# A build-time scheduler's durations set to traced ones, and wider gates for its vector banks

## The chip, the cores and the metric

The kernel runs on one core of a Trainium2 chip. The metric is the device time of one execution in microseconds. A difference is judged against the kernel before, run on the same chip. Five engines work side by side, each with its own in-order queue: TensorE (PE, matmuls), VectorE (DVE), ScalarE (ACT), GpSimd (POOL) and SyncE (SP, which issues transfers). They wait for each other through semaphores.

## The reference, cut to what matters

One transformer block with modulation: layer norm, attention with 32 heads of 16 over 2048 tokens, then a gated feed-forward. All inputs are bf16.

```python
mod = (silu(c) @ w_mod).reshape(1, 6, 1, 512)       # sa, ca, ga, sb, cb, gb
h = layernorm(x) * (1 + ca) + sa                    # x: 1 x 2048 x 512
q, k, v = split(h @ wqkv, 32 heads of 16)
p = softmax(q @ k.T * 16 ** -0.5)                   # 32 x 2048 x 2048
x = x + ga * ((p @ v) @ wo)
h = layernorm(x) * (1 + cb) + sb
x = x + gb * ((gelu(h @ w_gate) * (h @ w_up)) @ w_down)   # 512 -> 1792 -> 512
```

## The kernel before

**Tiling.** The scores are made transposed, keys on the 128 partitions and queries along the free dimension, in banks of 128 x 512 fp32. There are 32 x 2048 x 2048 / 65536 = 2048 such banks. `qk` writes them into six PSUM banks (`ps_sc`) used as two halves of three. Four matmuls of 32 rows (one for each of four heads) run side by side. The queries are cut into seven sets (`SETS`: 512, 512, 256, 256, 256, 128, 128), and a unit is one set and one of eight groups of four heads. `pv_round` multiplies four finished banks with the values and a column of ones into `ps_pv`, so that the row sums come out along with the products.

**Two ways for an exponential.** ScalarE takes two or three banks in one activation, `E<-ps_sc` with 1024 or 1536 elements. DVE can take a single bank, called a vector bank here, in the seven operations of `exp_vec`: `dt<-ps_sc` frees the PSUM bank; `dx<-dt` reads every second 16-bit word of `dt`; then come two `TENSOR_SCALAR`, two `TENSOR_TENSOR` and a last `SCALAR_TENSOR_TENSOR`. In the profile they write `ed`, `mreg` or `qT`, whose unused parts hold the results. Where a vector bank is taken, ScalarE's activation has 1024 elements in place of 1536.

**Side work.** Projections, output projection and feed-forward run in between as side work. They all go through a single PSUM bank (`ps_mi`), which DVE has to empty (L329, L334, L338) before the next group of matmuls may write it. The tanh of gelu runs on ScalarE (`wreg<-wreg`, 512 or 1024 elements, 37 times). When a unit has its last round, its sums go through DRAM (`scr_den`, `scr_rec`): SP issues a transfer out and one in, DVE takes the reciprocal (`rden<-den`), SP writes it out and issues four broadcasts into `rb`; DVE then multiplies (`onorm<-osb,rb`).

**What sets the order.** Every engine's order is fixed when the program is built. `rec` (L167) records each operation with the waits that it needs, and `model` (L244) gives it a start and an end in a planned time, from the durations of `cost` (L283); a transfer has its own durations in `model`. `probe` (L273) asks when an operation could start in that planned time. The loop in `stream` (L1069) decides with these planned times what PE does next: scores (`qk`), values (`pv_round`), a step of side work (`advance`), or a filler matmul that keeps PE busy. `background` (L986) and `step` hand DVE its next task when the plan says DVE is free. A wrong duration does not make a wrong result, since the semaphores hold; it makes another order.

**The gates of a vector bank** stand in `stream` (L1163 to L1166): fewer than `NACT` = 3 active ones, fewer than `BACK` = 8 DVE steps in the `backlog`, DVE planned free within 700 ns, and `credit`, the side work that is overdue in matmul columns, below 1024. `credit` grows with every group of scores and falls with each step of side work.

**The end.** `tail` (L1338) runs the feed-forward of the last two sets when all exponentials are given out. Before it, `side_ffn` with `EARLY` = 2 does the first two chunks of the second-last set (up-projection, tanh, product), and `near_end` (L841) forms the last sums on PE (`ps_mi<-osb,self`, `ps_sc<-osb,self`) with a reciprocal straight from PSUM (`rb<-ps_mi`, `rb<-ps_sc`). Then come the output projection of the last 128 tokens (`ps_sc<-wo,onorm`), its layer norm (`st<-ps_sc` and ten small operations), up- and down-projections and the last transfer out.

Of the kernel before, what the change touches and what calls it, by code (L numbers as in the profile page):

```python
# [38 lines left out]
CH = 3  # L39
# [6 lines left out]
NED = 6  # L46
LAG = 60
EARLY = 2
BACK = 8
SOON = 100  # L50
END = (0, None)

# [11 lines left out]
class _Op:  # L64
    __slots__ = ("eng", "stream", "seq", "fn", "inc", "waits", "clock", "tag", "t1")

    def __init__(self, eng, stream, seq, fn):
        self.eng = eng
        self.stream = stream
        self.seq = seq  # L70
        self.fn = fn
        self.inc = False
        self.waits = {}
        self.clock = None
        self.tag = None


class _Recorder:
# [88 lines left out]
    def rec(self, eng, fn, reads=(), writes=(), dma=None, cost=0.0):  # L167

        if self.dry:
            return None  # L170
        stream = eng if dma is None else "d_" + dma
        seq = self.count.get(stream, 0) + 1
        needs = {}

# [37 lines left out]
        if self.probing is not None:  # L212
            self.probing = max(self.probing, at)
            return None
        self.count[stream] = seq
        op = _Op(eng, stream, seq, fn)
        self.bystream.setdefault(stream, []).append(op)
        ck = self.clock[eng]
# [11 lines left out]
        for w, name, kind, bxs in acc:  # L230
            h = self.hist.setdefault(name, {})
            for b in bxs:
# [4 lines left out]
                else:  # L237
                    h.setdefault(b, [None, {}])[1][stream] = seq
        self.ops.append(op)
        self.model(op, max(at, self.free[eng]), cost)  # L240
        return op


    def model(self, op, t, cost):  # L244
        eng = op.eng
        if op.stream not in COMPUTE:
            self.free[eng] = t + 50
            self.dma_free = max(t + 1400, self.dma_free) + cost / 350
            op.t1 = self.dma_free + 1000
        elif eng == "pe":  # L250
            cols, rows, tp = cost
            mode = 0 if tp is None else (1 if rows == 32 else 2)
            t = max(t, self.pe_issue)
            if mode != self.pe_mode:
                t = max(t, self.pe_end + 105)
            q = range(16)
            if mode == 1:
                q = range(tp[0] // 8, tp[0] // 8 + 4)
            elif mode == 2:
                q = range(tp[1] // 32, 16, 4)  # L260
            t = max(t, max(self.tile_free[i] for i in q))
            end = t + max(cols, 64) / 2.4
            for i in q:
                self.tile_free[i] = end
            self.pe_mode, self.pe_issue, self.pe_end = mode, t + (4 if mode else 27), max(self.pe_end, end)
            self.free[eng] = t
            self.log.append((t, cols if mode == 0 else cols / 4))
            op.t1 = end + 158
        else:
            self.free[eng] = t + cost  # L270
            op.t1 = t + cost + (107 if eng == "act" else 92)
# [11 lines left out]
    def cost(self, eng, out, ins, kind):  # L283
        n = 1
        for _, k in (out if kind != "bn" else ins[0]).ap[1:]:
            n *= int(k)
        aps = [out] + list(ins)
        ps = any(self.kind.get(a.tensor.name) == "ps" for a in aps)
        small = all(mybir.dt.size(a.dtype) == 2 for a in aps)
        if eng == "act":  # L290
            return n * 0.833 + (60 if ps else 92)
        if eng == "pool":
            return n * 3.0 + 100
        f = 1
        if not ps:
            f = {("ts", True): 4, ("ts", False): 2, ("tt", True): 2}.get((kind, small), 1)
        return n * 1.042 / f + 65

    def mm(self, out, lhsT, rhs, start=True, stop=True, tp=None):
        n = 1  # L300
# [23 lines left out]
    def ts(self, eng, out, a, s1, s2, op0, op1=None):  # L324
        kw = {"op0": op0}
        if op1 is not None:
            kw["op1"] = op1
        rd = [a] + [s for s in (s1, s2) if isinstance(s, bass.AP)]
        return self.rec(eng, lambda e: e.tensor_scalar(out, a, s1, s2, **kw), rd, [out],  # L329
                        cost=self.cost(eng, out, [a], "ts"))  # L330

    def stt(self, out, a, s, b, op0, op1):
        rd = [a, b] + ([s] if isinstance(s, bass.AP) else [])
# [5 lines left out]

    def recip(self, out, in_):  # L340
        return self.rec("dve", lambda e: e.reciprocal(out, in_), [in_], [out],
                        cost=6.25 * self.cost("dve", out, [in_], "stt"))

    def memset(self, eng, ap, val, after=()):
        return self.rec(eng, lambda e: e.memset(ap, val), after, [ap], cost=self.cost(eng, ap, [], "ts"))
# [63 lines left out]
class _Kernel(_Recorder):  # L409
# [659 lines left out]
    def stream(self):  # L1069
# [39 lines left out]
        def take(n):  # L1109
            r, i = [], pos  # L1110
            while len(r) < n and i < nseq:
                if i not in vec:
                    r.append(i)
                i += 1
            return r, i
# [18 lines left out]
        while rp < len(rounds):  # L1134
# [5 lines left out]
            t = max(self.pe_now(), virt)  # L1140
# [7 lines left out]
            mem, after = take(CH - 1 if pos < nsplit + 12 and c % 2 else CH)  # L1148
# [5 lines left out]
            if tq is not None and tq <= t + 30:  # L1154
                slack = self.free["act"] - 600 - t
                w = self.next_side()
                if w is not None and pos >= w[1] and self.credit > 1536 and slack > 213 and self.probe(w[4][1]) <= t:
                    self.advance()
                    continue
                if self.short(t) > (0 if slack > 213 else DIRE) and slack > 0:  # L1160
                    self.mm(self.scp[:, s0, :], *filler)
                    continue
                g = None  # L1163
                if (('v', 3, 0) in self.have and len(active) < NACT and sum(v >= 4 * rp for v in vec) < NED
                        and self.backlog() < BACK and self.free["dve"] < t + 700
                        and len(mem) == CH and slack > -100 and self.credit < 1024):  # L1166
                    g = pos + CH * LEAD
                    g += 3 - g % 4
                    while g in vec:
                        g += 4  # L1170
                    if g >= nseq - 4 * LEAD or any(k not in self.have for k in self.keys(seq[g])):
                        g = None
                if g is not None:
                    vec.add(g)
                    mem, after = take(CH - 1)
                items = [(m, s0 + i) for i, m in enumerate(mem)]
                if g is not None:
                    items.append((g, s0 + len(mem)))
                self.require(sorted({k for m, _ in items for k in self.keys(seq[m])}))
                self.qk([(seq[m], k) for m, k in items])  # L1180
                n = len(mem)
                while self.step("act", self.free["act"]):
                    pass
                self.act(self.E[:, e0:e0 + n, :], self.scp[:, s0:s0 + n, :], ACT.Exp, scale=EXP_SCALE)
                for i, m in enumerate(mem):
                    owner[e0 + i] = rof[m]
                    self.slot[m] = self.E[:, e0 + i, :]
                if g is not None:
                    out = self.ED[pos >= ends[0]][nd % NED]
                    if pos < ends[0]:  # L1190
                        low.add(g)
                    steps = self.exp_vec(nd, self.scp[:, s0 + n, :], c % 2, out)
                    self.task(steps[:1], ("ld", nd), first=True)
                    self.task(steps[1:], ("exp", nd), self.after([("ld", nd)]))
                    active.append((("exp", nd), g, out))
                    nd += 1
                if self.work and pos >= self.work[0][1]:
                    w = self.work[0]
                    rate = w[3] / max(1, w[2] - pos)
                    self.credit = min(self.credit + rate * len(items), 4096)  # L1200
                pos, e, c = after, e0 + n, c + 1
                continue
# [4 lines left out]
            ts = None  # L1207
            side = False
            if w is not None and pos >= w[1]:
                ts = self.probe(w[4][1])  # L1210
                n = w[4][0]
# [13 lines left out]
            if self.short(t) > (0 if gap > 213 else DIRE) and not self.open and gap > 0 and self.probe(  # L1225
                    lambda: self.mm(self.mi[:, :], *filler)) <= t + 30:
                self.mm(self.mi[:, :], *filler)
                continue
            nxt = [x for x in (tq, tp[0], tp[1], ts) if x is not None and x > t + 30]
            if self.tasks:  # L1230
                nxt.append(max(self.free["dve"], t + 100))
# [251 lines left out]
```

## Time and profile before

| what | us |
|---|---|
| median of 3 runs | 917.43 (916.13 to 919.24) |
| the profiled execution | 915.94 |
| its span, first to last instruction | 914.2 |
| DVE busy | 817.3 (89%) |
| ScalarE (ACT) busy | 881.1 (96%) |
| PE busy | 798.2 (87%) |

The profile's rows are read like this. A group's row has the line, the engine, the operation, what it writes from what, the shape, and the count after an x; then the busy time of the group in us, the mean of one in ns, and the idle time before them with what ended it. A timeline's row has the start and the length in us. A row of the windows has the busy time of each engine in that stretch, and near its end the clock that TensorE was granted, as a share of full speed. An engine's instructions can overlap by some tenths of a microsecond, so the distance between two starts, not the length of one, is what an instruction costs its queue.

### The profile page before, as it was taken

What the parts mean: (1) busy time and instruction counts of PE and PEld (TensorE: products, weight loads), DVE (VectorE), ACT (ScalarE), POOL (GpSimd) and SP (SyncE); (2) the same over time, 40 slices, a digit from 0 to 9 for tenths busy, and PEclk for the clock granted to TensorE, in tenths of its full rate; (3) what the DMA queues carried; (4) which work ended last, traced back from release to release, by engine and by line L of the source; (5) the groups of instructions that cost most, each with busy time, mean ns of one, the idle gap of its engine ahead of it and who ended that gap; (6) DMA issues with size and microseconds to landing.
All of it is one profiled execution on the core that took longest, in us unless ns stands there. A gap on an engine that the chain in (4) does not pass through costs nothing.

```text
span 914.2 us, 20663 instructions
## 1 busy us (share of the span) xinstructions
PE 798.2 (87%) x8563; PEld 289.3 (32%) x8697; DVE 817.3 (89%) x2065; ACT 881.1 (96%) x754; POOL 3.6 (0%) x11
## 2 busy tenths in 40 slices
PE   8898888888888888888888888889888988898878
PEld 3332322222222222222223222333333333234455
DVE  8757999999997999999997997998999899988874
ACT  6999999999999999999999999999999999999991
POOL 1000000000000000000000000000000000000000
PEclk9999999999999999999999999999999999999999
DMA  9003210000100000000000000000000000000000
GB/s 299 1 24 94 101 47 14 13 14 13 54 13 13 2 13 15 13 14 25 9 25 14 14 8 14 14 26 19 9 15 19 16 12 12 22 15 14 23 6 13
DMA packets 35336, 25.18 MB, mean 28 GB/s; under 512 B 19053, under 2 KB 31082, under 8 KB 35242
## 3 DMA queue, kind: packets, MB, share of 16 engines
q1 hardware_dynamic: 32858, 22.28, 8.4%
q10 hardware_dynamic: 2384, 1.57, 0.6%
q8 instruction: 68, 1.11, 0.5%
q14 instruction: 26, 0.21, 0.1%
HBM read 21.23 MB, written 2.61 MB: 26 GB/s over the span
## 4 chain that ended last, share of the span: by engine, by line
DVE 43%; ACT 42%; PE 9%; DMA 3%; issue 2%; SPq 1%; DVEq 0%
ACT E L317 40%; DVE dt L329 7%; DVE dx L329 4%; PE ps_sc L304 4%; PE ps_mi L304 4%; DVE qT L321 3%; DVE qT L329 3%; DVE qT L334 3%; DVE ed L321 3%; DVE mreg L321 2%; DVE ed L334 2%; DVE mreg L334 2%; DVE ed L329 2%; DMA rb<-scr_rec 2%; DVE wreg L334 2%
## 5 line engine op out<-in xcount | busy, mean ns | idle before, releaser
L317 ACT ACTIVATE E<-ps_sc 128x1536 bf16<-128x1536 f32 (+2 forms) x698 | 852.7, 1390 | 13.8 <-PE ps_sc L304 13.0
L304 PE MATMUL ps_pv<-E,vaug 128*17 128x256 bf16 (+2 forms) x2922 | 182.6, 300 | 4.8 <-DVE osb L338 2.1
L304 PE MATMUL ps_sc<-qT,kme 32*128 32x256 bf16 (+2 forms) x1600 | 167.8, 304 | 21.3 <-ACT E L317 15.4
L304 PE MATMUL ps_sc<-qT,kmo 32*128 32x256 bf16 (+2 forms) x1664 | 167.6, 298 | 17.4 <-ACT E L317 12.6
L329 DVE TENSOR_SCALAR dt<-ps_sc 128x512 int32<-128x512 f32 x182 | 123.8, 682 | 10.4 <-PE ps_sc L304 9.5
L304 PE MATMUL ps_mi<-wreg,mreg 128*128 128x256 bf16 (+2 forms) x603 | 117.9, 306 | 11.9 <-DVE wreg L338 4.1
L304 PE MATMUL ps_sc<-kme,ident 128*128 128x512 bf16 x300 | 98.0, 383 | 32.9 <-ACT E L317 28.7
L304 PEld LDWEIGHTS ps_sc<-qT,kme 32*128 32x128 bf16 x1600 | 47.7, 92 | 130.6 <-ACT E L317 74.2
L304 PEld LDWEIGHTS ps_sc<-qT,kmo 32*128 32x128 bf16 x1664 | 49.4, 92 | 120.1 <-ACT E L317 66.7
L304 PEld LDWEIGHTS ps_pv<-E,vaug 128*17 128x17 bf16 x2922 | 53.4, 88 | 100.7 <-issue 86.7
L329 DVE TENSOR_SCALAR dx<-dt 128x512 f16<-128x512 uint16 x182 | 75.4, 418 | 0.1
L321 DVE TENSOR_TENSOR qT<-qT,dx 128x512 f16<-128x512 f16 x180 | 73.6, 416 | 1.2
L304 PEld LDWEIGHTS ps_mi<-wreg,mreg 128*128 128x128 bf16 x624 | 47.4, 97 | 61.8 <-issue 27.4
L334 DVE SCALAR_TENSOR_TENSOR qT<-dt,qT 128x512 int16<-128x512 int32 x90 | 61.5, 683 | 0.3
L304 PE MATMUL ps_mi<-dreg,hreg 128*128 128x512 bf16 x180 | 56.4, 384 | 3.2 <-issue 1.6
L321 DVE TENSOR_TENSOR ed<-ed,dx 128x512 f16<-128x512 f16 x124 | 51.0, 416 | 0.6
L304 PEld LDWEIGHTS ps_sc<-kme,ident 128*128 128x128 bf16 x342 | 24.9, 97 | 83.7 <-ACT E L317 77.2
L338 DVE CAST wreg<-ps_mi 128x512 bf16<-128x512 f32 x51 | 35.0, 685 | 16.7 <-PE ps_mi L304 16.5
L334 DVE SCALAR_TENSOR_TENSOR ed<-dt,ed 128x512 int16<-128x512 int32 x62 | 42.1, 681 | 0.4
L321 DVE TENSOR_TENSOR wreg<-wreg 128x512 bf16<-128x512 bf16 (+1 forms) x74 | 38.5, 520 | 0.9
L304 PE MATMUL ps_mi<-hreg,wreg 128*128 128x512 bf16 x107 | 35.0, 385 | 3.6 <-DVE qT L329 2.2
L334 DVE SCALAR_TENSOR_TENSOR wreg<-wreg,ps_mi 128x512 bf16<-128x512 bf16 x51 | 34.7, 680 | 1.8 <-PE ps_mi L304 1.5
(131 smaller groups left out, 740.8 us busy)
## 6 DMA issues: line engine op xcount, KB each, us to landing
rb<-scr_rec SPq DMA_DIRECT2D x64, 64.0 KB, 2.0
rb<-scr_rec SPq DMA_DIRECT2D x116, 32.0 KB, 1.8
mreg<-in_w_mod_dram SPq DMA_DIRECT2D x1, 2048.0 KB, 14.1
out_dram<-xs SPq DMA_DIRECT2D x16, 128.0 KB, 1.7
mreg<-in_B_w_gate_dram SPq DMA_DIRECT2D x4, 448.0 KB, 4.0
mreg<-in_B_w_up_dram SPq DMA_DIRECT2D x4, 448.0 KB, 6.1
dreg<-in_B_w_down_dram SPq DMA_DIRECT2D x3, 512.0 KB, 3.9
wreg<-in_A_wqkv_dram SPq DMA_DIRECT2D x3, 384.0 KB, 10.6
```

What stands on the lines that cost most here:

```text
L304: return self.rec("pe", lambda e: e.matmul(out, lhsT, rhs, start=start, stop=stop, tile_position=tp), [lhsT, rhs], [out], cost=(n, int(rhs ...
L317: return self.rec("act", lambda e: e.activation(out, in_, func, scale=scale, **kw), rd, wr, cost=self.cost("act", out, [in_], "act"))
L321: return self.rec(eng, lambda e: e.tensor_tensor(out, a, b, op), [a, b], [out], cost=self.cost(eng, out, [a, b], "tt"))
L329: return self.rec(eng, lambda e: e.tensor_scalar(out, a, s1, s2, **kw), rd, [out], cost=self.cost(eng, out, [a], "ts"))
L334: return self.rec("dve", lambda e: e.scalar_tensor_tensor(out, a, s, b, op0=op0, op1=op1), rd, [out], cost=self.cost("dve", out, [a, b], " ...
L338: return self.rec(eng, lambda e: e.tensor_copy(out, in_), [in_], [out], cost=self.cost(eng, out, [in_], "ts"))
```

## The change

It touches only numbers of the planner; no operation of the kernel has another form, and no transfer is added.

- `small` in `cost`: an operand counts as 16-bit and dense only if its last step is 1. Before, the type alone decided.
- ScalarE: 51 or 93 ns of fixed cost in place of 60 or 92.
- DVE: 68 ns of fixed cost in place of 65; a new kind `col` for an operation with scalars read per partition, planned at 0.52 ns an element and 190 ns from PSUM in 16 bit, 1.042 ns and 128 ns from PSUM otherwise, and at half rate in SBUF.
- The reciprocal: 360 ns less.
- Transfers: issuing on SP takes 430 ns in place of 50; the transfer starts 800 ns after the issue in place of 1400.
- Gates: `BACK` 10 in place of 8; `credit` below 2600 in place of 1024.

```diff
-BACK = 8
+BACK = 10
...
         if op.stream not in COMPUTE:
-            self.free[eng] = t + 50
-            self.dma_free = max(t + 1400, self.dma_free) + cost / 350
+            self.free[eng] = t + (430 if eng == "sp" else 50)
+            self.dma_free = max(t + 800, self.dma_free) + cost / 350
             op.t1 = self.dma_free + 1000
...
-        small = all(mybir.dt.size(a.dtype) == 2 for a in aps)
+        small = all(mybir.dt.size(a.dtype) == 2 and int(a.ap[-1][0]) == 1 for a in aps)
         if eng == "act":
-            return n * 0.833 + (60 if ps else 92)
+            return n * 0.833 + (51 if ps else 93)
         if eng == "pool":
             return n * 3.0 + 100
         f = 1
+        if ps and kind == "col":
+            return n * 0.52 + 190 if small else n * 1.042 + 128
         if not ps:
-            f = {("ts", True): 4, ("ts", False): 2, ("tt", True): 2}.get((kind, small), 1)
-        return n * 1.042 / f + 65
+            f = {("ts", True): 4, ("ts", False): 2, ("col", True): 2, ("tt", True): 2}.get((kind, small), 1)
+        return n * 1.042 / f + 68
...
-                        cost=self.cost(eng, out, [a], "ts"))
+                        cost=self.cost(eng, out, [a], "ts" if len(rd) == 1 else "col"))
...
-                        cost=6.25 * self.cost("dve", out, [in_], "stt"))
+                        cost=6.25 * self.cost("dve", out, [in_], "stt") - 360)
...
-                        and len(mem) == CH and slack > -100 and self.credit < 1024):
+                        and len(mem) == CH and slack > -100 and self.credit < 2600):
```

## The prediction

> **What bounds the kernel now.** I read the page's busy shares first, then the windows of the stretch between the first and the last softmax exponential, then ScalarE's groups by shape and its timeline, and last who waited for whom.
>
> ```profile
> span 914.2 us, 20663 instructions
> PE 798.2 (87%) x8563; PEld 289.3 (32%) x8697; DVE 817.3 (89%) x2065; ACT 881.1 (96%) x754; POOL 3.6 (0%) x11
> 15.26:888.59 873.33, 765.08 (x8259) 269.84 (x8386) 793.02 (x1996) 868.01 (x729) 0.31 (x1) 1.00 0.08 23
> 100.00:250.00 150.00, 129.82 (x1009) 39.23 (x1025) 148.46 (x366) 148.72 (x125) 0.00 (x0) 1.00 0.11 31
> 450.00:700.00 250.00, 221.63 (x2768) 78.76 (x2812) 227.88 (x575) 249.03 (x208) 0.00 (x0) 1.00 0.06 16
> ```
>
> In the window rows the columns are length, then busy time of PE, weight loads, DVE and ACT. ScalarE works 868.0 of the 873.3 us from first to last exponential; DVE has 873.3 - 793.0 = 80.3 us idle there, but almost none from 100 to 250. So the end is set by ScalarE's queue, plus a head of 15.3 us and a tail of 914.2 - 888.6 = 25.6 us. What ScalarE's queue holds:
>
> ```profile
> L317 ACT ACTIVATE E<-ps_sc 128x1536 bf16<-128x1536 f32 x482 | 688.3, 1525 | 4.0 <-PE ps_sc L304 3.4
> L317 ACT ACTIVATE E<-ps_sc 128x1024 bf16<-128x1024 f32 x210 | 229.3, 1105 | 1.2 <-PE ps_sc L304 1.0
> L317 ACT ACTIVATE wreg<-wreg 128x512 bf16<-128x512 bf16 x23 | 16.6, 722 | 0.0
> L317 ACT ACTIVATE wreg<-wreg 128x1024 bf16<-128x1024 bf16 x14 | 15.5, 1104 | 0.7 <-DVE wreg L321 0.7
> ```
>
> ```profile
> 15.26 3.71 ACT L317 ACTIVATE E<-ps_sc 128x1536 bf16<-128x1536 f32 x3 [0.58 <-PE ps_sc L304]
> ...
> 879.32 5.57 ACT L317 ACTIVATE E<-ps_sc 128x1536 bf16<-128x1536 f32 x4
> 884.64 0.76 ACT L317 ACTIVATE wreg<-wreg 128x512 bf16<-128x512 bf16 x1
> ...
> 886.50 0.76 ACT L317 ACTIVATE wreg<-wreg 128x512 bf16<-128x512 bf16 x1
> 887.01 1.58 ACT L317 ACTIVATE E<-ps_sc 128x1536 bf16<-128x1536 f32 x1
> ```
>
> Instructions on ScalarE overlap, so the mean of one is not what it costs the queue. Four 1536-wide ones from 879.32 to 884.64 are 5.32 / 4 = 1.330 us each, 0.195 less than their mean. The 1024-wide one, 420 ns shorter in the mean, is 0.910 us; the tanh of 512 takes 887.01 - 886.50 = 0.51, that of 1024 by the same overlap 0.91. The queue's work is 482 x 1.330 + 210 x 0.910 + 23 x 0.51 + 14 x 0.91 = 856.6 us. The stretch lasts 873.3, so 16.7 us are lost to exponentials that start late. Those 16.7 and the count of banks are all that the planner can move in this stretch.
>
> ```profile
> ACT E L317 <- PE ps_sc L304: 4.4, 12, 0.6
> PE ps_mi L304 <- DVE wreg L334: 6.6, 14, 0.8
> PE ps_mi L304 <- DVE xw L321: 4.6, 12, 0.7
> PE ps_mi L304 <- DVE wreg L338: 4.1, 11, 0.7
> DVE onorm L321 <- DMA rb<-scr_rec: 5.9, 9, 1.3
> ```
>
> ```profile
> 147.21 0.74 DVE L329 TENSOR_SCALAR kmo<-ps_mi,rm 128x512 bf16<-128x512 f32 x1
> 148.00 0.40 PE L304 MATMUL ps_mi<-wreg,hreg 128*128 128x128 bf16 x4 [0.72 <-DVE kmo L329]
> 148.77 2.79 ACT L317 ACTIVATE E<-ps_sc 128x1536 bf16<-128x1536 f32 x2 [0.54 <-PE ps_sc L304]
> ```
>
> The waits (us in all, times, longest) say where a visible part comes from, and the three rows at 148 show one whole case. PE's queue is in order. The planner put projection matmuls where it thought DVE had already emptied the one side bank; DVE had not, PE stood 0.72 us, the scores behind it were late, and ScalarE stood 0.54 us.
>
> **The change part by part.** Planned durations first. One vector bank is seven DVE operations, and here seven run without a gap:
>
> ```profile
> 156.22 0.68 DVE L329 TENSOR_SCALAR dt<-ps_sc 128x512 int32<-128x512 f32 x1
> 156.82 0.68 DVE L334 SCALAR_TENSOR_TENSOR mreg<-dt,mreg 128x512 int16<-128x512 int32 x1
> 157.41 0.42 DVE L321 TENSOR_TENSOR mreg<-mreg,dx 128x512 f16<-128x512 f16 x1
> 157.75 0.42 DVE L329 TENSOR_SCALAR dx<-dt 128x512 f16<-128x512 uint16 x1
> 158.09 0.28 DVE L329 TENSOR_SCALAR mreg<-mreg 128x512 f16<-128x512 f16 x1
> 158.29 0.28 DVE L329 TENSOR_SCALAR mreg<-dx 128x512 f16<-128x512 f16 x1
> 158.49 0.42 DVE L321 TENSOR_TENSOR mreg<-mreg,dx 128x512 f16<-128x512 f16 x1
> 158.82 0.68 DVE L329 TENSOR_SCALAR dt<-ps_sc 128x512 int32<-128x512 f32 x1
> ```
>
> From 156.22 to 158.82 they cost 2.60 us of queue. The old formulas add up to 2 x 598.5 + 3 x 198.4 + 2 x 331.7 = 2456 ns, because the strided read of dx is planned at 198 ns and takes 158.09 - 157.75 = 340. The new ones give 2 x 601.5 + 334.8 + 2 x 201.4 + 2 x 334.8 = 2610. So each vector bank made DVE about 0.15 us later than planned, 182 x 0.15 = 27 us in all, and now about 0.01 early. The key copies with a column scalar (kmo) were planned at 598 and take 0.66 between starts (147.21 to the next, 147.87), now planned at 661.
>
> The gates. In the changed program's own order ScalarE has 475 exponentials of 1536 and 217 of 1024: 7 more banks go to DVE, 189 in place of 182. (The new durations with the old gates would plan only 170; the gates more than win back what honest prices cost.)
>
> - ScalarE's queue: 7 x (1.330 - 0.910) = 2.9 us less. It lies on the path. Term: -2.9.
> - DVE: 7 x 2.60 = 18.2 us more, covered by its idle 80.3, of which about 80.3 - 18.2 - 2.9 = 59 remain. Without cover each bank would cost 2.60 against the 0.42 it saves. Of the short exponentials, the first 200 ScalarE banks have 40 (37 before), the next 700 have 85 (88), the rest 92 (85): the added ones stand where DVE has room, not in the full stretch.
>  ScalarE's visible idle is 1.28 us of 150 where DVE is 99% busy and 0.97 of 250 where it is 91%: 0.85% against 0.39%, or 0.06 points for each point of DVE idle given up. From 9.2% to 6.8% idle that is 0.14% of 870 = 1.2 us. Bounds 0 (the added banks sit in gaps) and 2.9 (DVE as full everywhere as at 100 to 250: 0.85% less the mean 0.61% is 2.1 visible, times 1.4 for overlap lost). I take +1.0.
> - Late evacuations. ScalarE waits visibly for scores 12 times, 4.4 us; each also forfeits the 0.195 overlap, 6.7 us in all. With planned and traced DVE times equal, cases like 148 should be planned around. Bounds: 0 (the waits come from other unknowns) and -10 (60% of all 16.7). I take 60% of the 6.7, since the three largest of PE's waits for DVE (6.6 + 4.6 + 4.1 = 15.3 us) are such hand-overs of the side bank: -4.0.
> - Transfers. The chain from a reciprocal to its broadcast in rb was planned at 2.4 + 0.06 + 2.4 + up to 0.75 us; it is now 1.8 + 0.06 + 3 x 0.43 + 1.8 + up to 0.2, that is 5.0 to 5.2 in place of 5.3 to 5.6. Nothing is issued that was not before, SP's queue keeps its count and nearly its order. The row of a broadcast is
>
> ```profile
> rb<-scr_rec SPq DMA_DIRECT2D x116, 32.0 KB, 1.8
> ```
>
>  and 1.8 is what the new formula says. Term 0, bounds 0 and the rival below.
> - Head: the order up to the first exponentials is unchanged. Term 0.
>
> The tail is moved though not edited. The last two tanh and the up-projection chunk behind them stand about one exponential later: before, the second-last item on ScalarE is a tanh and the last an exponential; now a tanh comes after the last exponential.
>
> ```profile
> 886.42 1.07 PE L304 MATMUL ps_mi<-wreg,mreg 128*128 128x128 bf16 x16
> ...
> 889.50 0.40 PE L304 MATMUL ps_pv<-E,vaug 128*17 128x128 bf16 x16
> ...
> 892.08 2.80 PE L304 MATMUL ps_sc<-wo,onorm 128*128 128x512 bf16 x7
> ```
>
> ```profile
> 888.14 0.29 DVE L321 TENSOR_TENSOR onorm<-osb,rb 128x128 bf16<-128x128 f32 x1 [1.32 <-DMA rb<-scr_rec]
> 888.35 0.68 DVE L334 SCALAR_TENSOR_TENSOR wreg<-wreg,ps_mi 128x512 bf16<-128x512 bf16 x1
> ...
> 889.61 0.96 DVE L341 RECIPROCAL rb<-ps_mi 128x128 f32<-128x128 f32 x1
> 890.48 0.23 DVE L338 COPY osb<-ps_pv 128x128 f32<-128x128 f32 x1
> ...
> 891.47 0.96 DVE L341 RECIPROCAL rb<-ps_sc 128x128 f32<-128x128 f32 x1 [0.57 <-PE ps_sc L304]
> ```
>
> ```profile
> 892.00:894.00 2.00, 2.00 (x6) 0.50 0.00 0
> ```
>
> Count from the end of the last exponential, 887.01 + 1.58 = 888.59. Before, the product of that chunk starts at -0.24, held by the broadcast (1.32 us of wait), and the second reciprocal starts at +2.88. Now the 16 last value matmuls (0.40) and the chunk's 16 matmuls (1.07) come first, so the product starts near +1.5; then both reciprocals follow without the copy and the 0.57 wait between them: the first 1.26 behind the product's start (889.61 - 888.35), the second 0.87 later (890.48 - 889.61), near +3.6. That is 0.75 late; PE's output matmuls, which run back to back, start about 0.35 late. I take +0.5. Bounds: +1.2 (0.75 and two more down matmuls of 0.2 ahead of the last output ones), and -1.1: those output matmuls take 2.80 / 7 = 0.40 at a granted clock of 0.50 (the last row), and twice the clock would win 8 x 0.2 = 1.6.
>
> The Trainium skill ("TensorE: Matmul & The Clock Gate", section "What's actually happening") says that the clock falls to half after an idle window of about 3.4 us. The 0.50 agrees with it; with the new matmuls filling that window the rule would leave the clock whole, and the sum below would be 1.6 us lower. The window's phase is not to be known, so the row's clock stays.
>
> Sum: -2.9 + 1.0 - 4.0 + 0.5 = -5.4. The profiled execution took 915.94 (span 914.2 and 1.7 around it), so 910.5 on its scale. It is 1.5 below the median of the three runs, 917.43; on the median's scale I forecast 912.0.
>
> **The rivals.** *Waits mostly vanish.* If the 0.15 us per bank was behind most of the 16.7, 10 go: -2.9 - 10 + 1.0 + 0.5 = -11.4, 906.0. For it: DVE is full where the waits are. Against: the listed waits of ScalarE are 4.4.
>
> *It does nothing that counts.* The planner only reshuffles, as many new hand-overs are late as old ones repaired: -2.9 + 1.0 + 0.5 = -1.4, 916.0. For it: any edit of a price moves thousands of instructions. Against: the error repaired is one-sided, DVE always later than planned.
>
> *Slower: DVE parks on broadcasts.* The planner now counts on a landing 0.2 to 0.45 us earlier. DVE is in order, so a product queued too early holds the loads of vector banks and evacuations behind it, and PE and ScalarE in turn. Nine of 51 products wait now, 5.9 / 9 = 0.66 us each; were it all, 42 x 0.66 = 28 us; if as much of them reaches ScalarE as now of PE's waits (4.4 of 15.3), +8. With no repair and the late tail: -2.9 + 1.0 + 8 + 1.2 = +7.3, 924.7. It decides from about 20 parked products more. For it: the wait of 1.32 at 888.14. Against: the median landing of 1.8 is the planned one.
>
> **How the numbers follow.** Forecast 0.45, vanishing waits 0.17, nothing 0.20, slower 0.18. The measurement tells about 0.3% (2.75 us) from no change. Faster (below 914.7): 0.62; within: 0.20; slower (above 920.2): 0.18. The range 905 to 921 takes in the second and third and the milder half of the last. The forecast's own range is 907.5 to 914.5.
>
> **What would show it.** In the changed kernel: 475 and 217 exponentials and 189 loads of dt; a last exponential ending near 883 (888.6 - 6); lost time in the stretch near 14 in place of 16.7 us; fewer and shorter waits of PE for wreg, xw and kmo; DVE busy near 835; a tail of 25 to 27 us. I am wrong if lost time grows beyond 19, if onorm waits for rb pass 15 us, or if the tail exceeds 28.

## The result, and the profile after

The changed kernel took 910.33 us (median of 6 runs, 908.93 to 913.2) beside 917.22 us (6 runs, 915.58 to 919.24) for the kernel before on the same chip. The ratio is 0.9929, with a 95% interval of 0.9909 to 0.9948: it is 0.7% faster. The profiled execution took 911.24, of which 909.4 is span. It lies 0.9 above the median of its kernel's runs, and the profiled execution of before (915.94) 1.3 below that of its own. So the two profiles are 4.7 us apart where the medians are 6.9 apart, and the parts that are read from the profiles below add up to the smaller figure.

The head of the page after, with the span and the busy time of each engine:

```profile
span 909.4 us, 20886 instructions
PE 826.3 (91%) x8708; PEld 292.0 (32%) x8708; DVE 833.9 (92%) x2114; ACT 877.2 (96%) x754; POOL 3.6 (0%) x11
```

DVE has 16.6 us more work, ScalarE 3.9 less. PE's busy time isn't to be compared: before, the profile has 8697 weight loads but only 8563 matmuls, so matmul records are missing; after, both counts are 8708.

The windows after (length, then PE, weight loads, DVE, ACT), from the first to the last exponential and in the same two stretches as before:

```profile
16.66:882.46 865.80, 791.35 (x8384) 271.58 (x8383) 808.26 (x2040) 863.61 (x729) 0.31 (x1) 1.00 0.08 23
100.00:250.00 150.00, 134.20 (x1043) 38.47 (x1044) 146.63 (x357) 150.00 (x127) 0.00 (x0) 1.00 0.12 34
450.00:700.00 250.00, 230.92 (x2835) 81.11 (x2834) 238.55 (x608) 250.00 (x211) 0.00 (x0) 1.00 0.07 16
```

ScalarE's visible idle time is gone from both inner stretches: 150.00 of 150 and 250.00 of 250, where 148.72 and 249.03 stood before. From 100 to 250 DVE is less busy than it was (146.63 against 148.46), and from 450 to 700 more (238.55 against 227.88).

ScalarE's groups by shape, and its timeline at both ends of that stretch:

```profile
L319 ACT ACTIVATE E<-ps_sc 128x1536 bf16<-128x1536 f32 x475 | 690.2, 1580 | 2.3 <-PE ps_sc L306 1.9
L319 ACT ACTIVATE E<-ps_sc 128x1024 bf16<-128x1024 f32 x217 | 245.9, 1160 | 0.1
L319 ACT ACTIVATE wreg<-wreg 128x512 bf16<-128x512 bf16 x23 | 16.8, 731 | 0.4 <-DVE wreg L323 0.3
L319 ACT ACTIVATE wreg<-wreg 128x1024 bf16<-128x1024 bf16 x14 | 16.4, 1173 | 0.0
```

```profile
16.66 9.34 ACT L319 ACTIVATE E<-ps_sc 128x1536 bf16<-128x1536 f32 x8 [0.58 <-PE ps_sc L306]
...
880.93 1.53 ACT L319 ACTIVATE E<-ps_sc 128x1536 bf16<-128x1536 f32 x1
882.26 0.70 ACT L319 ACTIVATE wreg<-wreg 128x512 bf16<-128x512 bf16 x1
```

The means have grown (1580 ns after 1525) though the work is the same: the shortest and the median distance from one 1536-wide start to the next are 1.330 and 1.331 us in both traces. So only starts may be compared. The prediction's prices hold: the shortest distances of the four forms, in its order, are 1.330, 0.904, 0.52 and 0.95 us, where it had 1.330, 0.910, 0.51 and 0.91. With its prices the queue between first and last exponential holds 475 x 1.330 + 217 x 0.910 + 22 x 0.51 + 14 x 0.91 = 853.2 us (one tanh now stands behind the last exponential). The stretch is 882.46 - 16.66 = 865.8 long, so 12.6 us are lost in place of 16.7.

| part, us | before | after | difference | forecast |
|---|---|---|---|---|
| head, to the first exponential | 15.3 | 16.7 | +1.4 | 0 |
| ScalarE's work in the stretch | 856.6 | 853.2 | -3.4 (0.5 of it is the tanh) | -2.9 |
| lost to late exponentials | 16.7 | 12.6 | -4.1 | +1.0 - 4.0 |
| tail, behind the last exponential | 25.6 | 26.9 | +1.3 | +0.5 |
| span | 914.2 | 909.4 | -4.8 | -5.4 |

The waits between the two ends:

```profile
DVE onorm L323 <- DMA rb<-scr_rec: 7.7, 13, 1.2
PE ps_mi L306 <- DVE wreg L340: 3.9, 9, 0.7
PE ps_mi L306 <- DVE wreg L336: 2.2, 7, 0.7
ACT E L319 <- PE ps_sc L306: 1.9, 6, 0.6
PE ps_mi L306 <- DVE xw L323: 1.6, 5, 0.5
```

PE's three hand-over waits that came to 15.3 us come to 7.7, and ScalarE waits visibly 6 times and 1.9 us where it waited 12 times and 4.4.

### The profile page after: what moved, and what is told of

The parts are those of the page before. It is cut to its first block, busy times and chain, and to the rows that moved or that the text cites. A ratio compares the mean times of both kernels' runs of the same rounds, so it can differ in the third digit from the quotient of the medians.

```text
span 909.4 us, 20886 instructions
## 1 busy us (share of the span) xinstructions
PE 826.3 (91%) x8708; PEld 292.0 (32%) x8708; DVE 833.9 (92%) x2114; ACT 877.2 (96%) x754; POOL 3.6 (0%) x11
## 4 chain that ended last, share of the span: by engine, by line
ACT 83%; PE 6%; DVE 5%; DMA 4%; SPq 1%; issue 0%; DVEq 0%
ACT E L319 81%; PE ps_sc L306 3%; ACT wreg L319 2%; PE ps_mi L306 2%; DMA rb<-scr_rec 1%; DMA scr_rec<-rden 1%; SPq L369 1%; DMA mreg<-in_w_mod_dram 1%; PE ps_pv L306 1%; DMA den<-scr_den 0%; DVE qT L323 0%; DVE qT L336 0%; DVE dx L331 0%; DVE wreg L323 0%; DVE wreg L340 0%
## 5 line engine op out<-in xcount | busy, mean ns | idle before, releaser
L306 PE MATMUL ps_sc<-kme,ident 128*128 128x512 bf16 x334 | 106.7, 384 | 35.5 <-ACT E L319 32.0
L331 DVE TENSOR_SCALAR dt<-ps_sc 128x512 int32<-128x512 f32 x189 | 129.6, 687 | 5.7 <-PE ps_sc L306 3.0
L331 DVE TENSOR_SCALAR dx<-dt 128x512 f16<-128x512 uint16 x189 | 78.2, 420 | 0.1
L323 DVE TENSOR_TENSOR qT<-qT,dx 128x512 f16<-128x512 f16 x188 | 77.0, 419 | 0.7
L336 DVE SCALAR_TENSOR_TENSOR qT<-dt,qT 128x512 int16<-128x512 int32 x94 | 64.4, 686 | 0.4
L306 PE MATMUL ps_mi<-dreg,hreg 128*128 128x512 bf16 x210 | 62.7, 384 | 0.8 <-DVE wreg L336 0.3
L306 PEld LDWEIGHTS ps_sc<-kme,ident 128*128 128x128 bf16 x334 | 22.6, 97 | 90.4 <-ACT E L319 87.7
L306 PE MATMUL ps_mi<-hreg,wreg 128*128 128x512 bf16 x120 | 39.4, 386 | 0.7 <-DVE qT L331 0.2
L306 PE MATMUL ps_mi<-wo,onorm 128*128 128x512 bf16 x120 | 35.3, 384 | 1.4 <-DVE xw L323 1.3
```

What stands on the lines that cost most here:

```text
L306: return self.rec("pe", lambda e: e.matmul(out, lhsT, rhs, start=start, stop=stop, tile_position=tp), [lhsT, rhs], [out], cost=(n, int(rhs ...
L323: return self.rec(eng, lambda e: e.tensor_tensor(out, a, b, op), [a, b], [out], cost=self.cost(eng, out, [a, b], "tt"))
L336: return self.rec("dve", lambda e: e.scalar_tensor_tensor(out, a, s, b, op0=op0, op1=op1), rd, [out], cost=self.cost("dve", out, [a, b], " ...
```

## The experiments

Every run below is read as the changed kernel was: its count of banks and tanh priced as in the prediction, against its own stretch. "Lost" and "tail" come from one profile each; the times are medians, and the ratios go against the kernel before on the same chip. Beside the four groups of runs the kernel before took 917.22, 915.94, 915.51 and 916.65 us, so kernels of different groups are best compared by their ratios.

| kernel | DVE durations | vector banks | lost | tail | time | ratio (95%) |
|---|---|---|---|---|---|---|
| before | old | 182 | 16.7 | 25.6 | 917.22 | 1 |
| changed | new | 189 | 12.6 | 26.9 | 910.33 | 0.9929 (0.9909 to 0.9948) |
| changed, again | new | 189 | 12.4 | 27.0 | 908.78 | 0.9929 (0.9913 to 0.9946) |
| gates only | old | 195 | 21.0 | 31.0 | 921.64 | 1.0064 (1.0042 to 1.0085) |
| durations only, old gates | new | 170 | 12.0 | 24.9 | 915.03 | 0.9988 (0.9976 to 1.0001) |
| DVE's durations and gates | new | 191 | 12.1 | 30.9 | 912.48 | 0.9960 (0.9947 to 0.9973) |
| all but DVE's durations | old | 193 | 18.0 | 34.8 | 921.41 | 1.0062 (1.0040 to 1.0084) |
| DVE's durations, gates, guard | new | 188 | 12.6 | 25.8 | 908.10 | 0.9918 (0.9903 to 0.9933) |
| strided read and gates only | strided read new | 189 | 14.4 | 39.4 | 923.35 | 1.0085 (1.0067 to 1.0102) |
| changed, strided read old | strided read old | 197 | 21.7 | 31.3 | 919.95 | 1.0046 (1.0029 to 1.0062) |
| gates only, guard | old | 191 | 21.0 | 25.7 | 916.16 | 0.9996 (0.9984 to 1.0007) |
| strided read overpriced, guard | 0.11 us too long | 178 | 12.6 | 24.9 | 912.46 | 0.9964 (0.9951 to 0.9977) |
| changed, guard | new | 186 | 16.0 | 24.0 | 909.92 | 0.9935 (0.9916 to 0.9953) |
| wider gates, guard | new | 191 | 16.0 | 25.4 | 911.35 | 0.9951 (0.9935 to 0.9967) |

### Gates without durations, and durations without gates

Of the kernel before, only the gates are widened:

```diff
-BACK = 8
+BACK = 10
-                        and len(mem) == CH and slack > -100 and self.credit < 1024):
+                        and len(mem) == CH and slack > -100 and self.credit < 2600):
```

> Old durations, new gates (BACK 10, credit below 2600): 195 vector banks planned. Theory (honest DVE durations are what cut the lost time): 13 banks fewer for ScalarE are 13 x 0.42 = -5.5 us, but the time lost to late exponentials stays at 16.7 or grows to about 20, because DVE is later than planned 195 times; 913 to 917 us. Rival (the gates alone do it, durations do not matter): lost time 12 to 14, 908 to 911 us.

Measured: 921.64 us, slower than either theory said. ScalarE had 13 banks less to do and still its stretch was only 2.2 us shorter, because 21.0 us were lost; and the tail grew to 31.0, which is the larger part of the loss (5.4 us against 4.3). So the gates alone are not what made the change fast. The other half alone, the changed kernel with the old gates:

```diff
-BACK = 10
+BACK = 8
-                        and len(mem) == CH and slack > -100 and self.credit < 2600):
+                        and len(mem) == CH and slack > -100 and self.credit < 1024):
```

> New durations, old gates (BACK 8, credit below 1024): 170 vector banks planned. Theory: 12 more banks for ScalarE are +5.0 us, lost time falls from 16.7 to about 12 or less; 915 to 919 us, about the kernel before. Rival (durations do not matter): lost time as before, 921 to 924 us.

Measured: 915.03 us, lost 12.0. The planner gives ScalarE 12 banks more, and the 4.7 us of lost time that go pay for them. Each half alone wins nothing that a user would notice, or loses; together they win 0.7%.

### Which durations

The changed kernel with ScalarE's and the transfers' old numbers, and its complement, the kernel before with the new gates and only ScalarE's and the transfers' numbers new. First:

```diff
-            self.free[eng] = t + (430 if eng == "sp" else 50)
-            self.dma_free = max(t + 800, self.dma_free) + cost / 350
+            self.free[eng] = t + 50
+            self.dma_free = max(t + 1400, self.dma_free) + cost / 350
-            return n * 0.833 + (51 if ps else 93)
+            return n * 0.833 + (60 if ps else 92)
```

> The changed kernel with the old numbers for ScalarE and for transfers; only DVE's durations and the gates are new: 191 vector banks. Theory: DVE's durations carry it, so lost time 11 to 14 and 908 to 912 us. Rival (transfers or ScalarE's numbers matter): lost time above 16, 914 us or more.

Measured: lost 12.1, as the theory has it, and 912.48 us, 0.5 above its range; what it lacks against the changed kernel is its tail of 30.9. The complement has these lines the other way round on the kernel before, beside the gates:

> The complement: old DVE durations, new numbers for ScalarE and transfers, new gates: 193 vector banks. Theory: like the gates alone, lost time 16 to 20, 913 to 917 us. Rival: lost time 12 to 14, 908 to 911 us.

Measured: lost 18.0, as expected, but 921.41 us, slower than expected: its tail is 34.8, and in its profile the head too is long (17.6). So DVE's durations cut the lost time, and the other numbers do little for it. The count of vector banks is not what does it: at 191 banks 12.1 us are lost here with DVE's new durations, and 21.0 with the old ones in a kernel further down. Of DVE's durations, only the strided read, on the kernel before with the new gates:

```diff
-        small = all(mybir.dt.size(a.dtype) == 2 for a in aps)
+        small = all(mybir.dt.size(a.dtype) == 2 and int(a.ap[-1][0]) == 1 for a in aps)
```

> Of the durations only the strided read's is new (dx at 335 ns in place of 198), with the new gates: 189 vector banks. Theory: this is 0.14 of the 0.155 us that a bank was short, so lost time 12 to 15 in place of the 21.0 with old durations; the last two tanh both stand behind the last exponential, so the tail is 30 to 32 and the time 912 to 916 us. Rival (the column scalars and fixed costs matter as much): lost time 17 or more, 917 us or more.

Measured: lost 14.4, as expected, but 923.35 us, because the tail was 39.4 and not 30 to 32: the first tanh behind the last exponential waits 8.82 us for DVE there. And the changed kernel with that one line as it was before:

> The changed kernel with the strided read at its old 198 ns, all else new: 197 vector banks. Theory: lost time 17 to 21, tail 30 to 33 (both tanh behind the last exponential): 916 to 921 us. Rival: lost time 12 to 15, 911 to 914 us.

Measured: 919.95 us and a tail of 31.3, as the theory said, and lost 21.7, a little above its 17 to 21. ScalarE's waits for PE in the two, from 15.3 to 882 us; first with the strided read's new duration alone, then with every new duration but that:

```profile
ACT E L317 <- PE ps_sc L304: 3.7, 10, 0.9
```

```profile
ACT E L319 <- PE ps_sc L306: 9.1, 21, 1.4
```

A part of the second figure came by way of TensorE's clock, which was granted at half from 443 to 449 us (the third figure from the end):

```profile
443.00:449.00 6.00, 5.96 (x40) 1.15 (x40) 4.32 (x12) 3.95 (x4) 0.00 (x0) 0.50 0.09 26
```

From 440 to 452 us 3.1 us were lost there, in every other profile at most 0.8. All six timings of this kernel have a mean granted clock of 0.992 to 0.994, so the fall seems to be of its order and not of one execution; whether a hand-over that the price made late set it off was not shown. So one duration, 198 ns where the trace has 340, carries 6 to 7 us of lost time: 21.0 to 14.4 on the kernel before with the new gates, and 21.7 to 12.6 on the changed kernel, of which about 3 is that stretch. All the other numbers together are worth about 2 once that one is right (14.4 to 12.6), and nothing that shows without it (21.0 and 21.7).

### The tail

The tail of 30.9 us in the third kernel is read from ScalarE's timeline there:

```profile
870.94 8.24 ACT L319 ACTIVATE E<-ps_sc 128x1536 bf16<-128x1536 f32 x6
882.55 0.63 ACT L319 ACTIVATE wreg<-wreg 128x512 bf16<-128x512 bf16 x1 [3.37 <-DVE wreg L323]
883.67 0.63 ACT L319 ACTIVATE wreg<-wreg 128x512 bf16<-128x512 bf16 x1 [0.49 <-DVE wreg L323]
```

The last exponential ends at 879.18, and both tanh of the two early feed-forward chunks come behind it, the first after 3.37 us of waiting. The gate lets vector banks through while `credit`, the overdue side work, is as high as 2600, and at the end there is no time left to catch up. A guard closes the gate earlier for the last 160 banks; here it is on that third kernel:

```diff
-                        and len(mem) == CH and slack > -100 and self.credit < 2600):
+                        and len(mem) == CH and slack > -100 and self.credit < (2600 if pos < nseq - 160 else 1024)):
```

> The kernel with only DVE's durations and the gates new (912.5, tail 30.9), and near the end (last 160 banks) the credit gate back at 1024: 188 vector banks. Theory now: the durations cut the lost time, and what is left between that kernel and the changed one (910.3) is the tail, into which the two early feed-forward chunks spilled. So lost time 11 to 13, tail 25 to 27.5, 907 to 910 us. Rival (the transfers' and ScalarE's numbers win their 2 us elsewhere): tail shorter or not, 911.5 us or more.

Measured: 908.10 us, lost 12.6, tail 25.8, as the theory said. ScalarE's timeline with the guard:

```profile
879.33 0.77 ACT L319 ACTIVATE wreg<-wreg 128x512 bf16<-128x512 bf16 x1
879.85 1.60 ACT L319 ACTIVATE E<-ps_sc 128x1536 bf16<-128x1536 f32 x1
881.18 0.77 ACT L319 ACTIVATE wreg<-wreg 128x512 bf16<-128x512 bf16 x1
```

One tanh is ahead of the last exponential again and neither waits. So the numbers for transfers and ScalarE won the changed kernel its 2 us over the third kernel by the order that they happened to give near the end. This is the fastest version here, but its interval overlaps the changed kernel's, and its five timings all had a granted clock of 0.999 or 1.000, the changed kernel's six 0.996 to 0.998. At 1.000 the changed kernel's repeat, on the same chip, has 908.81, so nothing is left between the two. The same guard on the gates-only kernel, to take tail and lost time apart:

> Old durations and new gates as in the gates-only kernel (921.6), with the credit gate back at 1024 for the last 160 banks: 191 vector banks. Theory: the guard takes the spilled tail away (25 to 27 us in place of 31), the old durations keep the lost time at 18 to 21 us: 914 to 918 us, 6 to 9 us above the same gates and guard with DVE's durations new (908.1). Rival (the gates-only kernel was slow through its tail alone): lost time 14 or less, 907 to 911 us.

Measured: 916.16 us, tail 25.7, lost 21.0, as the theory said. With gates and guard alike, and on two chips, DVE's durations are worth 0.8%: ratios of 0.9996 and 0.9918. The clock does not explain it: eight of twelve timings had 1.000 here, four of five there, and none less than 0.998. Waits in the two from 15.3 to 882 us, first with the old durations, then with DVE's new ones:

```profile
ACT E L317 <- PE ps_sc L304: 7.2, 24, 0.6
PE ps_mi L304 <- DVE wreg L338: 5.9, 17, 0.7
PE ps_mi L304 <- DVE wreg L334: 4.4, 12, 1.0
PE ps_mi L304 <- DVE kmo L329: 2.5, 6, 0.7
```

```profile
PE ps_mi L306 <- DVE wreg L336: 3.7, 8, 1.0
PE ps_mi L306 <- DVE wreg L340: 3.2, 9, 0.5
ACT E L319 <- PE ps_sc L306: 2.8, 9, 0.6
```

The hand-over of `kmo` that made the case at 148 in the prediction is a row of 2.5 us in the first and has no row among the waits of PE in the second.

### A price that is too high

The guarded kernel with the strided read planned at 449 ns:

```diff
-            f = {("ts", True): 4, ("ts", False): 2, ("col", True): 2, ("tt", True): 2}.get((kind, small), 1)
+            f = {("ts", True): 4, ("ts", False): 1.4, ("col", True): 2, ("tt", True): 2}.get((kind, small), 1)
```

> The kernel of 908.1 with the strided read planned at 449 ns, 0.11 us above the traced 0.34: 178 vector banks. Theory (only being later than planned costs lost time; being earlier costs only banks): 10 banks more for ScalarE than at 188 are +4.2 us, lost time 9.5 to 12.5, tail 25 to 26.5: 910.5 to 913.5 us. Rival (a wrong price costs on either side): lost time 15 or more, 915 us or more.

Measured: 912.46 us, lost 12.6. The time is as expected, by the 10 banks; the lost time does not fall below that of the honest price (I allowed 9.5 to 12.5). At these two sizes, a price 0.14 us too low costs lost time, a price 0.11 us too high costs only banks.

### The rest: the guard on the changed kernel, wider gates, a repeat

> The changed kernel with the same guard for the last 160 banks: 186 vector banks. Theory: tail 25 to 26.5 in place of 27.0, lost time 11.5 to 13.5, 3 banks more for ScalarE +1.3: 908 to 911 us, about the changed kernel. It also gives one more head with the new transfer numbers (16.7 and 17.2 in the changed kernel's two profiles, 15.1 to 15.3 with the old numbers): below 16 if those were chance.

Measured: 909.92 us, tail 24.0, but lost 16.0, a miss. Up to the last 160 banks the order is that of the changed kernel, so most of it belongs to the one execution, which was the slowest of its six, 2.5 us above the median. The waits from 80 to 95 us, and the clock in two stretches:

```profile
ACT E L319 <- PE ps_sc L306: 1.6, 3, 1.0
DVE onorm L323 <- DMA rb<-scr_rec: 0.9, 1, 0.9
```

```profile
89.00:92.00 3.00, 3.00 (x15) 0.65 (x13) 0.96 (x4) 1.77 (x2) 0.00 (x0) 0.53 0.89 305
202.00:205.00 3.00, 3.00 (x14) 0.60 (x13) 2.37 (x6) 2.19 (x3) 0.00 (x0) 0.50 0.02 5
```

A broadcast landed 0.9 us after DVE reached its product, and ScalarE waited 1.6 us there, where the changed kernel's profile has 0.6. TensorE's clock was at half there and again at 202 us; the changed kernel's two profiles have it whole in both stretches. From 80 to 96 and from 198 to 210 us this profile lost 4.6 us, those two 1.4 and 1.5. So these two falls of the clock are nearly all of the 3.4 us by which 16.0 exceeds 12.6. The timed runs give the changed kernel's ratio.

```diff
-BACK = 10
+BACK = 12
-                        and len(mem) == CH and slack > -100 and self.credit < (2600 if pos < nseq - 160 else 1024)):
+                        and len(mem) == CH and slack > -100 and self.credit < (4000 if pos < nseq - 160 else 1024)):
```

> The kernel of 908.1 (DVE's durations new, guard) with still wider gates, BACK 12 and credit below 4000: 191 vector banks. Theory: 3 more banks -1.3 us, with honest durations the lost time stays at 11.5 to 13.5, tail 24.5 to 27: 906 to 909 us. Rival (DVE is full by now): lost time 15 or more or tail 28 or more, 911 us or more.

Measured: 911.35 us, lost 16.0: the rival's figures. Three more banks are 1.3 us less for ScalarE, 3.4 more are lost. From 550 to 860 us DVE stood once for 3.6 us, waiting for sums to come back:

```profile
DVE rden L343 <- DMA den<-scr_den: 3.6, 1, 3.6
```

That transfer is not most of it: around it, from 845 to 860 us, ScalarE lost 1.2 us where the 908.1 us kernel lost 0.2, while from 550 to 700 us it lost 4.1 against 2.0. That the fuller DVE is behind the rest was not shown. The repeat of the changed kernel:

> The changed kernel again, for a second profile: is the head of 16.7 us (before: 15.3) its own or one execution's, and do lost time and tail repeat? Theory: the order up to the first exponential is the same, so a head of 15.0 to 16.0, lost time 11.5 to 13.5, tail 26 to 28, 909 to 911.5 us. Rival: the head stays at 16.5 or more.

Measured: 908.78 us, lost 12.4, tail 27.0; these repeat. The head was 17.2, the rival's figure and not 15.0 to 16.0. The repeat also shows that the gain is not the clock's: the three of its timings with a granted clock of 1.000 have a median of 908.81 us, the seven such timings of the kernel before on the same chip 914.61. ScalarE's timeline in that repeat:

```profile
7.83 0.63 ACT L319 ACTIVATE xw<-xs 128x512 bf16<-128x512 bf16 x1 [2.67 <-DMA xs<-in_A_x_dram]
...
17.19 1.45 ACT L319 ACTIVATE E<-ps_sc 128x1536 bf16<-128x1536 f32 x1 [0.58 <-PE ps_sc L306]
```

The second part of x landed late. The 14 profiles have heads of 15.1 to 15.7 us, but for three: 16.7 and 17.2 in the changed kernel's two, and 17.6 in the kernel with all new numbers but DVE's durations. What sets these three apart is TensorE's clock. From 12 to 14 us, first before, then after:

```profile
12.00:14.00 2.00, 1.87 (x8) 0.52 (x7) 1.60 (x5) 1.42 (x3) 0.00 (x0) 1.00 1.10 337
```

```profile
12.00:14.00 2.00, 2.00 (x6) 0.58 (x6) 1.89 (x5) 1.12 (x3) 0.00 (x0) 0.50 1.10 337
```

In the other two it is 0.54 and 0.61, in the remaining ten profiles 1.00. The eight matmuls `ps_sc<-hreg,wreg` of that stretch took 2.38 us before and 3.50 after:

```profile
11.67 2.38 PE L304 MATMUL ps_sc<-hreg,wreg 128*128 128x512 bf16 x8
```

```profile
11.95 3.50 PE L306 MATMUL ps_sc<-hreg,wreg 128*128 128x512 bf16 x8
```

Ahead of the fall PE stood in one piece for 1.34, 1.74 and 1.99 us in these three, and for 1.08 at most in the others; after, it waited for a load:

```profile
9.69 0.66 PE L306 MATMUL ps_sc<-sc_bf,mreg 128*128 128x1 bf16 x21 [1.34 <-DMA mreg<-in_w_mod_dram]
```

The order of every engine up to the first exponential is the same in all kernels here, as far as the records go, and three more profiles with the new transfer numbers have heads of 15.1, 15.2 and 15.7. So a long head belongs to the execution, not to the change. Why the loads land late in some executions is open.

## Why the prediction was right

- **ScalarE's queue, -2.9.** Right: 475 and 217 exponentials were profiled.
- **Head, 0.** Right as to the change; the +1.4 of the profile belongs to that execution, and 1.1 of it to the clock (3.50 against 2.38). That the profiles' -4.8 comes so near to -5.4 is in part luck: without the longer head it would be -6.2. The medians are 6.9 apart, with 4.8 to 8.3 as their interval, so the forecast lies inside it.
- **Late evacuations, -4.0.** Right in place and nearly in size: without the gates the new durations took the lost time from 16.7 to 12.0, that is -4.7. Counted start by start against the shortest distance of each form, the starts behind a visible wait (over 0.15 us) lost 7.0 us before and 2.7 after; all other starts, none of them more than 0.4 us late, lost 10.0 before and 10.3 after. So what went is what the prediction took the term from, the visible waits with their overlap, and the rest stayed. That the strided read is the price that matters was shown by changing it alone, both ways.
- **Fuller DVE, +1.0.** Near in size with the new durations: from 12.0 at 170 banks to 12.4 and 12.6 at 189, though one profile at 191 has 16.0 with its clock whole in the stretch. It would have been far off with the old ones: 16.7 at 182 banks became 21.0 at 191 and 195. The prediction took the two terms as independent; they are not. A vector bank costs lost time when its price is too low.
- **The tail, +0.5.** Mis-sized: +1.3. The working had the chunk's product held by PE at 1.5 us behind the last exponential and the second reciprocal at 3.6. DVE's timeline after, where the last exponential ends at 882.46:

```profile
884.37 0.29 DVE L323 TENSOR_TENSOR onorm<-osb,rb 128x128 bf16<-128x128 f32 x1 [1.12 <-DMA rb<-scr_rec]
884.58 0.68 DVE L336 SCALAR_TENSOR_TENSOR wreg<-wreg,ps_mi 128x512 bf16<-128x512 bf16 x1
...
886.79 0.90 DVE L343 RECIPROCAL rb<-ps_sc 128x128 f32<-128x128 f32 x1
```

 The broadcast held it again, for 1.12 us, so the product started at 884.58 - 882.46 = 2.12 and the second reciprocal at 4.33. The step took the broadcast as out of the way because PE would be later; it had moved with the rest.

```profile
887.00:889.00 2.00, 2.00 (x6) 0.50 0.00 0
```

 The granted clock was at half again under the output matmuls, as the row of before had it. The whole clock that the rule of the Trainium skill ("TensorE: Matmul & The Clock Gate", section "What's actually happening") might have given did not come. The idle window of about 3.4 us that the rule asks for is in neither trace: PE's longest waits there were 1.27 us before and 1.40 after, so the prediction's reading that the row agrees with the rule holds for the half only. In six of the other profiles the clock stayed whole there, as in the guarded kernel:

```profile
886.00:888.00 2.00, 2.00 (x11) 0.89 (x10) 1.06 (x3) 0.02 (x1) 0.00 (x0) 1.00 0.00 0
```

 Its first six output matmuls took 1.46 us against 2.48 in the changed kernel. So the whole clock that the prediction kept as a lower bound does come in other orders. Five of those six tails are 24.0 to 25.8, and the sixth is the spilled one of 31.0.
- **Transfers, 0, and the slower rival.** DVE's products waited 7.7 us in 13 waits for broadcasts, below the 15 that the prediction named, after 5.9 in 9. The rival fell. The numbers for transfers and ScalarE were not neutral, though: through the order near the end they decided about 4 us of tail (26.9 against 30.9), and with DVE's old durations as much the other way (34.8 against 31.0).
- **Vanishing waits, and nothing that counts.** A good 12 us of lost time stay whatever the durations are, also when the strided read is overpriced. The small delays without a visible wait are 9 to 11 us of it in each of the 14 profiles. What holds them was not tried.

What the prediction did not see is that one half of the change, the gates, is harmful without the other: +0.6% with the old durations. With the guard it is neutral there (0.9996), since the guard takes the spilled tail away and the lost time of 21.0 stays.

## What to carry to other kernels

A planner that hands out work by planned durations should have them from start-to-start distances in a trace, and the one to look for first is the price that is too low in an operation repeated many times: here 0.14 us in one of seven operations cost 6 to 7 us. Tune gates and limits only after the prices, since a gate tuned on wrong prices hides them: these gates cost 0.6% with the old prices and gave 0.6% (ratios 0.9988 to 0.9929) with the new. Look at the granted clock before a difference of 2 or 3 us between two profiles is put down to an edit: here it made three long heads, and about 3 us of lost time in two profiles. Look at what a greedy gate leaves for the end, where nothing can cover it.

## What the runs showed of the hardware

A strided 16-bit read in SBUF takes VectorE 0.34 us between starts for 512 elements, where a dense one takes 0.20.

The length of TensorE's waits alone does not tell when its granted clock falls to half. In the changed kernel's tail it was 0.65 and 0.50 in the 4 us from 885, right behind waits of 0.43 and 1.40 us; with wider gates and guard 0.58 and 0.56 behind 0.67 and 0.82; but in the guarded kernel it stayed at 1.00 behind 1.02 and 0.78. The timings follow the clock: of the 17 of the kernel before on one chip, the two at a mean granted clock of 1.000 took 914.0 and 914.2 us, and the one at 0.994 took 920.2.
